# Sums over partitions: ones matmuls in place of a GpSimd operation

## The chip, the cores and the metric

The kernel runs on one core of a Trainium2 chip. The metric is the time of one execution on the device in microseconds. The engines are TensorE (PE: matmuls, and its weight loads, PEld), VectorE (DVE), ScalarE (ACT), GpSimd (POOL) and SyncE (SP), which here issues every DMA.

## The reference

Three stages follow each other: a decaying linear attention gives x (1536 tokens of 512), a mixture of 8 experts that is run densely for every token, and a last feed-forward layer with a leaky activation. Only the gate of the second stage matters here:

```python
logits = x @ w_gate                       # 1536 x 8
P = np.exp(logits - logits.max())
for _ in range(8):
    P /= P.sum(1, keepdims=True) + 1e-09  # over the 8 experts
    P /= P.sum(0, keepdims=True) + 1e-09  # over the 1536 tokens
    P *= N / E
for e in range(E):
    out += P[:, e:e+1] * (np.maximum(x @ w1[e], 0.0) @ w2[e])
```

## The kernel before

Tokens go in three blocks of 512. All engines work through their instructions in the order in which the code is written (a manual schedule); tiles from pools carry the waits. PSUM has a pool of seven banks under one tag (`bank`).

After the attention the loop runs over ten "experts" e (the eight real ones, and the last layer as two more) and the blocks b. `l1(e, b)` does eight tiles f of layer 1: 12 matmuls each, in three precisions (`mm3`: high by high, low by high, high by low), into a bank `a`; then ACT writes `hh` (the high half) and VectorE `hl` (the low half), which frees the bank. `l2T(e, b)` then sums over the eight tiles f into four banks `o`, 12 matmuls for each f; VectorE multiplies `o` by `pb`, the gate's row of this expert spread over all partitions.

Weights come from DRAM into `raw` (four slots), and `split_w` makes their halves: `wh` on ACT, `wl` on GpSimd (L98). The first three are split on VectorE during the attention. The next five belong to expert 0 and are split at tiles 0, 2, 4 and 6 of `l1(0, 0)` and tile 0 of `l2T(0, 0)` (the list `early`). Each split also issues a later weight load on SP's queue.

The gate is worked out beside `l1(0, 0)` and `l2T(0, 0)`. A list `side` holds its steps, and after each tile f one step is taken: `gate(2)`, `transposes`, then eight times `sink_iter`, two empty steps, and `sink_end` with `load_pb(0)`, so that the last falls behind tile 4 of `l2T(0, 0)`. The logits P lie as 128 partitions x 8 experts x 12 token groups, so a sum over tokens is a sum along the free dimension (VectorE, tile `s`) and then one over the partitions. The latter, and the maximum at the start (`mg` from `m`), are a custom operation of GpSimd, `partition_all_reduce` (L305, L321). `sink_end` transposes P on TensorE (`pt`, L335), writes it to DRAM (`pdram`) and reads back `pb`.

Of the kernel before, what the change touches and what calls it, by code (L numbers as in the profile page):

```python
# [8 lines left out]

F32 = mybir.dt.float32  # L10
# [4 lines left out]
ALU = mybir.AluOpType  # L15
AX = mybir.AxisListType
# [8 lines left out]
E, F = 8, 1024  # L25
# [10 lines left out]
def tile_kernel(ctx, tc, qkT, kv, cmask, ctab, w_gate, w1, w2, w_in, w_out, alpha, out):  # L36
    nc = tc.nc
# [3 lines left out]
    const = ctx.enter_context(tc.tile_pool(name="const", bufs=1))  # L41
# [10 lines left out]
    def bank(name):  # L52
        return psp.tile([128, 512], F32, tag="ps", name=name)

    ident = const.tile([128, 128], F32, name="ident")
    al = const.tile([128, FF // 128], F32, name="al")
    wg = const.tile([128, KD, E], F32, name="wg")
    wgs = const.tile([128, KD, 2 * E], F32R, name="wgs")
# [2 lines left out]
    Pt = const.tile([E * NT, 128], F32, name="Pt")  # L61
    pdram = drp.tile([E * NT, 128], F32, name="pdram")

    # ------------------------------------------------------------ weights
    srcs = []
    for e in range(E):
        srcs += [(1, w1[e][:, 256 * p:256 * p + 256]) for p in range(4)]
# [44 lines left out]
        xl[b] = xp.tile([128, KD, TB], F32R, tag=f"xl{b}", name=f"xl{b}_{gen}")  # L112

    with tc.manual_schedule():
        # -------------------------------------------------------- attention
        with ExitStack() as actx:
            ap_ = actx.enter_context(tc.tile_pool(name="attn", bufs=2))
            ld = actx.enter_context(tc.tile_pool(name="ld", bufs=3))
# [34 lines left out]
            for t in T:  # L153
                nc.gpsimd.memset(t, 0.0)
            make_identity(nc, ident)
            nc.gpsimd.memset(ebias, -896.0 * 2.0 ** 23)

            def scores(i):
# [92 lines left out]
            def gate(blk):  # L251
                if blk == 0:
                    lgT.append(gpool.tile([128, N], F32, tag="pb", name="lgT"))
                ps = bank(f"gt{blk}")
                for k in range(KD):
                    nc.tensor.matmul(ps[:16, :], wgs[:, k, :], xh[blk][:, k, :], start=(k == 0), stop=False)
                    nc.tensor.matmul(ps[:16, :], wgs[:, k, :], xl[blk][:, k, :], start=False, stop=(k == KD - 1))
                nc.scalar.activation(out=lgT[0][:16, TB * blk:TB * blk + TB], in_=ps[:16, :], func=AF.Copy)
# [6 lines left out]
            for i in range(NST):  # L265
# [16 lines left out]
                if i == 3:  # L282
                    nc.scalar.activation(out=wgs[:, :, 0:E], in_=wg, func=AF.Copy)
                    nc.gpsimd.tensor_tensor(
                        out=wgs[:, :, E:2 * E], in0=wg, in1=wgs[:, :, 0:E].bitcast(F32), op=ALU.subtract
                    )

        # -------------------------------------------------------- experts
        mp = ctx.enter_context(tc.tile_pool(name="mp", bufs=1))
        tp = ctx.enter_context(tc.tile_pool(name="tp", bufs=2))  # L290
        sp = ctx.enter_context(tc.tile_pool(name="sp", bufs=1))
        hh_t, hl_t, acc, pb = {}, {}, {}, {}

        def transposes():
            ps = bank("lgt")
            for t in range(NT):
                nc.tensor.transpose(ps[:, 16 * t:16 * t + 16], lgT[0][:16, C * t:C * t + C], ident[:16, :16])
            lg = sp.tile([128, NT * 16], F32, tag="lg", name="lg")
            nc.scalar.activation(out=lg, in_=ps[:, :NT * 16], func=AF.Copy)
            v = lg.rearrange("p (t e) -> p e t", e=16)  # L300
            nc.vector.tensor_tensor(out=P, in0=v[:, 0:E, :], in1=v[:, E:2 * E, :], op=ALU.add)
            m = sp.tile([128, 1], F32, tag="m", name="m")
            nc.vector.tensor_reduce(out=m, in_=P, axis=AX.XY, op=ALU.max)
            mg = sp.tile([128, 1], F32, tag="mg", name="mg")
            nc.gpsimd.partition_all_reduce(mg, m, channels=128, reduce_op=ReduceOp.max)  # L305
            nm = sp.tile([128, 1], F32, tag="nm", name="nm")
            nc.vector.tensor_scalar_mul(nm, mg, -1.0)
            nc.scalar.activation(out=P, in_=P, func=AF.Exp, bias=nm)

        def sink_iter(it):  # L310
            r = sp.tile([128, NT], F32, tag="r", name=f"r{it}")
            nc.vector.tensor_reduce(out=r, in_=P.rearrange("p e t -> p t e"), axis=AX.X, op=ALU.add)
            nc.vector.tensor_scalar_add(r, r, 1e-9)
            nc.vector.reciprocal(out=r, in_=r)
            nc.vector.tensor_tensor(
                out=P, in0=P, in1=r.unsqueeze(1).to_broadcast([128, E, NT]), op=ALU.mult
            )
            s = sp.tile([128, E], F32, tag="s", name=f"s{it}")
            nc.vector.tensor_reduce(out=s, in_=P, axis=AX.X, op=ALU.add)
            g = sp.tile([128, E], F32, tag="g", name=f"g{it}")  # L320
            nc.gpsimd.partition_all_reduce(g, s, channels=128, reduce_op=ReduceOp.add)  # L321
            nc.vector.tensor_scalar_add(g, g, 1e-9)  # L322
            nc.vector.reciprocal(out=g, in_=g)  # L323
            nc.vector.scalar_tensor_tensor(  # L324
                out=P,
                in0=P,
                scalar=float(N // E),
                in1=g.unsqueeze(2).to_broadcast([128, E, NT]),
                op0=ALU.mult,
                op1=ALU.mult,  # L330
            )

        def sink_end():
            ps = bank("pt")
            nc.tensor.transpose(ps[:E * NT, :128], P.rearrange("p e t -> p (e t)"), ident)  # L335
            nc.scalar.activation(out=Pt, in_=ps[:E * NT, :128], func=AF.Copy)
            nc.sync.dma_start(out=pdram, in_=Pt)

        def load_pb(e):
            pb[e] = gpool.tile([128, N], F32, tag="pb", name=f"pb{e}")  # L340
            nc.sync.dma_start(
                out=pb[e],
                in_=pdram[NT * e:NT * e + NT, :].rearrange("t p -> (t p)").partition_broadcast(128),
            )
# [35 lines left out]
        side = []  # L380
# [116 lines left out]
        for i in range(3, 8):  # L497
            early.append(i)
        side.append(lambda: gate(2))
        side.append(transposes)  # L500
        for it in range(8):
            side.append(lambda it=it: sink_iter(it))
        side += [lambda: None] * 2
        side.append(lambda: (sink_end(), load_pb(0)))

        todo = list(range(32))
# [83 lines left out]
```

## Time and profile before

| | |
|---|---|
| median of 3 runs | 1428.52 us (1428.16 to 1431.36) |
| profiled execution: span from first to last instruction | 1426.4 us |
| what lies around the span, by the median | 2.1 us |
| TensorE busy | 1372.0 us, 96% of the span |
| VectorE, ACT, GpSimd busy | 410.0, 269.8 and 395.2 us |
| mean granted clock of TensorE | 0.980 |
| DMA | 91.01 MB, q1 19.0% of 16 engines' span |

The profiled execution has no other time of its own than its span. In the timelines below, a row has the start in us, the duration, the engine, the line, the operation, what it writes and reads, and in brackets how long the engine was idle before it and what ended that. Matmuls overlap, so their durations are longer than the distance between two of them.

### The profile page before, as it was taken

The page shows a single profiled execution, that of the slowest core. Times are in us where ns is not written, and L with a number is a line of the kernel's source. Part 1 is how long each engine was busy: PE and PEld are TensorE (multiplying, and loading weights), DVE is VectorE, ACT ScalarE, POOL GpSimd, SP SyncE. Part 2 cuts the span into 40 slices and gives each one's busy share as a digit, 9 for nine tenths or more (in the row PEclk, how much of TensorE's full clock was granted, in tenths as well). Part 3 has the DMA queues.
Part 4 walks back from the last instruction along what each step waited for, and adds up shares of the span by engine and source line. Part 5 has one row for each costly group of instructions (what it writes and reads, how often), then busy time and mean ns, then how long its engine had stood idle before and what let it go on. Part 6 is the DMA issues. An engine that isn't in the chain of part 4 may idle for free.

```text
span 1426.4 us, 15358 instructions
## 1 busy us (share of the span) xinstructions
PE 1372.0 (96%) x6465; PEld 1130.2 (79%) x6465; DVE 410.0 (29%) x683; ACT 269.8 (19%) x396; POOL 395.2 (28%) x260
## 2 busy tenths in 40 slices
PE   9971899999999999999999999999999999999999
PEld 7750688888888888888888888888888888888887
DVE  5512211342143233314421432311112212233322
ACT  1310112111211221121122112211212321132100
POOL 4311004013410431241134105312412462264211
PEclk9985899999999999999999999999999999999999
DMA  9400003311321231033113212300310120010000
GB/s 330 167 29 29 24 1 104 118 52 33 123 67 52 75 125 45 30 103 119 52 34 121 67 52 74 111 1 1 103 37 0 45 74 0 0 60 1 30 30 30
DMA packets 46548, 91.01 MB, mean 64 GB/s; under 512 B 3504, under 2 KB 20240, under 8 KB 46480
## 3 DMA queue, kind: packets, MB, share of 16 engines
q1 hardware_dynamic: 46480, 90.04, 19.0%
q8 instruction: 50, 0.82, 0.2%
q14 instruction: 18, 0.15, 0.0%
HBM read 78.44 MB, written 11.58 MB: 63 GB/s over the span
## 4 chain that ended last, share of the span: by engine, by line
PE 89%; DVE 0%; issue 0%
PE a L105 15%; PE a L106 15%; PE a L104 15%; PE o L104 12%; PE o L105 12%; PE o L106 12%; PE o L494 3%; PE o L495 3%; PE o L493 3%; PE pt L335 0%; DVE y L470 0%; DVE P L324 0%; DVE g L323 0%; DVE g L322 0%
## 5 line engine op out<-in xcount | busy, mean ns | idle before, releaser
L104 PE MATMUL a<-xh,wh 128*128 128x512 f32 x960 | 373.7, 389 | 0.0
L106 PE MATMUL a<-xh,wl 128*128 128x512 f32 x960 | 373.5, 389 | 0.0
L105 PE MATMUL a<-xl,wh 128*128 128x512 f32 x960 | 373.5, 389 | 0.0
L106 PE MATMUL o<-hh,wl 128*128 128x512 f32 x768 | 302.2, 393 | 15.5 <-POOL wl L98 15.5
L104 PE MATMUL o<-hh,wh 128*128 128x512 f32 x768 | 302.6, 394 | 7.3 <-DVE hl L395 7.3
L105 PE MATMUL o<-hl,wh 128*128 128x512 f32 x768 | 302.0, 393 | 0.0
L98 POOL TENSOR_TENSOR wl<-raw,wh 128x1024 fp32r<-128x1024 f32 x77 | 183.9, 2389 | 294.2 <-ACT wh L97 259.5
L443 POOL TENSOR_TENSOR acc<-acc,t 128x512 f32<-128x512 f32 x84 | 105.8, 1291 | 507.1 <-DVE t L442 507.1
L394 ACT ACTIVATE hh<-a 128x512 fp32r<-128x512 f32 x192 | 112.3, 596 | 518.3 <-PE a L106 518.2
L104 PEld LDWEIGHTS a<-xh,wh 128*128 128x128 f32 x960 | 180.2, 188 | 37.7 <-issue 0.2
L106 PEld LDWEIGHTS a<-xh,wl 128*128 128x128 f32 x960 | 180.2, 188 | 37.5
L105 PEld LDWEIGHTS a<-xl,wh 128*128 128x128 f32 x960 | 180.2, 188 | 37.4
L395 DVE SCALAR_TENSOR_TENSOR hl<-a,hh 128x512 fp32r<-128x512 f32 x192 | 129.8, 688 | 246.0 <-ACT hh L394 246.0
L106 PEld LDWEIGHTS o<-hh,wl 128*128 128x128 f32 x768 | 146.2, 190 | 47.1 <-POOL wl L98 16.4
L104 PEld LDWEIGHTS o<-hh,wh 128*128 128x128 f32 x768 | 146.1, 190 | 38.8 <-DVE hl L395 8.4
L105 PEld LDWEIGHTS o<-hl,wh 128*128 128x128 f32 x768 | 146.2, 190 | 30.5
L442 DVE TENSOR_TENSOR t<-o,pb 128x512 f32<-128x512 f32 x84 | 57.9, 692 | 388.5 <-PE o L106 329.6
L97 ACT ACTIVATE wh<-raw 128x1024 fp32r<-128x1024 f32 x80 | 84.4, 1055 | 149.6 <-PE o L105 130.5
L409 POOL TENSOR_TENSOR hl<-g,hh 128x512 fp32r<-128x512 f32 x48 | 62.1, 1294 | 139.1 <-ACT hh L408 138.9
L494 PE MATMUL o<-wl,hh 128*128 128x512 f32 (+1 forms) x200 | 76.1, 381 | 0.0
L495 PE MATMUL o<-wh,hl 128*128 128x512 f32 (+1 forms) x200 | 76.1, 380 | 0.0
L493 PE MATMUL o<-wh,hh 128*128 128x512 f32 (+1 forms) x200 | 76.1, 380 | 0.0
(70 smaller groups left out, 573.6 us busy)
## 6 DMA issues: line engine op xcount, KB each, us to landing
raw<-in_w_dram SPq DMA_DIRECT2D x64, 512.0 KB, 3.5
rd<-in_w_in_dram SPq DMA_DIRECT2D x16, 512.0 KB, 3.7
wd<-q SPq DMA_DIRECT2D x32, 256.0 KB, 2.2
rd<-in_w_out_dram SPq DMA_DIRECT2D x16, 512.0 KB, 3.7
raw<-wd SPq DMA_DIRECT2D x16, 512.0 KB, 3.2
qk<-in_qkT_dram SPq DMA_DIRECT2D x12, 512.0 KB, 6.8
kv<-in_kv_dram SPq DMA_DIRECT2D x12, 512.0 KB, 5.7
pb<-pdram SPq DMA_DIRECT2D x8, 768.0 KB, 4.4
```

What stands on the lines that cost most here:

```text
L97: nc.scalar.activation(out=hi, in_=t, func=AF.Copy)
L98: eng.tensor_tensor(out=lo, in0=t, in1=hi.bitcast(F32), op=ALU.subtract)
L104: nc.tensor.matmul(ps, wh, xh, start=first, stop=False)
L105: nc.tensor.matmul(ps, wh, xl, start=False, stop=False)
L106: nc.tensor.matmul(ps, wl, xh, start=False, stop=last)
L394: nc.scalar.activation(out=hi, in_=ps, func=AF.Relu)
L395: nc.vector.scalar_tensor_tensor(out=lo, in0=ps, scalar=0.0, in1=hi.bitcast(F32), op0=ALU.max, op1=ALU.subtract)
L409: nc.gpsimd.tensor_tensor(out=lo, in0=g, in1=hi.bitcast(F32), op=ALU.subtract)
L443: nc.gpsimd.tensor_tensor(out=acc[b][:, d, :], in0=acc[b][:, d, :], in1=t, op=ALU.add)
L493: nc.tensor.matmul(ps, hh_, wh, start=first, stop=False)
L494: nc.tensor.matmul(ps, hh_, wl, start=False, stop=False)
L495: nc.tensor.matmul(ps, hl_, wh, start=False, stop=last)
```

## The change

The custom operation is gone. `ones`, a 128 x 128 matrix of ones, is filled on VectorE at the start. A sum over partitions is now a matmul of `ones` with the partial sums, whose result in PSUM has the total in every partition. For the maximum, VectorE multiplies the identity by `m` (`dm`, a diagonal matrix), the matmul spreads all 128 values over each partition, and VectorE takes the maximum of them. The iteration is cut at the matmul: `rows` is what leads up to `s`, `cols` begins with the matmul and ends with the `rows` of the next iteration. The list `side` is now `gate(2)`, `transposes`, `shift`, eight times `cols`, and `sink_end`, without empty steps.

```diff
+    ones = const.tile([128, 128], F32, name="ones")
...
+            nc.vector.memset(ones, 1.0)
...
-            mg = sp.tile([128, 1], F32, tag="mg", name="mg")
-            nc.gpsimd.partition_all_reduce(mg, m, channels=128, reduce_op=ReduceOp.max)
+            dm = sp.tile([128, 128], F32, tag="dm", name="dm")
+            nc.vector.tensor_scalar(out=dm, in0=ident, scalar1=m, scalar2=None, op0=ALU.mult)
+            sums["m"] = dm
+
+        def shift():
+            ps = bank("mx")
+            nc.tensor.matmul(ps[:, 0:128], ones, sums["m"], start=True, stop=True)
             nm = sp.tile([128, 1], F32, tag="nm", name="nm")
-            nc.vector.tensor_scalar_mul(nm, mg, -1.0)
+            nc.vector.tensor_reduce(out=nm, in_=ps[:, 0:128], axis=AX.X, op=ALU.max)
+            nc.vector.tensor_scalar_mul(nm, nm, -1.0)
             nc.scalar.activation(out=P, in_=P, func=AF.Exp, bias=nm)
+            rows(0)
 
-        def sink_iter(it):
+        def rows(it):
...
             nc.vector.tensor_reduce(out=s, in_=P, axis=AX.X, op=ALU.add)
+            sums[it] = s
+
+        def cols(it):
+            ps = bank(f"cs{it}")
+            nc.tensor.matmul(ps[:, 0:E], ones, sums[it], start=True, stop=True)
             g = sp.tile([128, E], F32, tag="g", name=f"g{it}")
-            nc.gpsimd.partition_all_reduce(g, s, channels=128, reduce_op=ReduceOp.add)
-            nc.vector.tensor_scalar_add(g, g, 1e-9)
+            nc.vector.tensor_scalar_add(g, ps[:, 0:E], 1e-9)
             nc.vector.reciprocal(out=g, in_=g)
...
+            if it < 7:
+                rows(it + 1)
...
         side.append(transposes)
+        side.append(shift)
         for it in range(8):
-            side.append(lambda it=it: sink_iter(it))
-        side += [lambda: None] * 2
+            side.append(lambda it=it: cols(it))
         side.append(lambda: (sink_end(), load_pb(0)))
```

In GpSimd's queue, from the last weight split that comes ahead of the gate, this stood before (rows named ISA without a tile are set-up instructions of the operation that follows):

```order
L98 TENSOR_TENSOR wl_755<-raw_452,wh_754 128x1024
L305 ISA
L305 ISA mg<-m 128x1
L98 ISA
L98 TENSOR_TENSOR wl_828<-raw_512,wh_827 128x1024
L321 ISA
L321 ISA g_840<-s_838 128x8
L321 ISA g_869<-s_867 128x8
L98 ISA
L98 TENSOR_TENSOR wl_892<-raw_610,wh_891 128x1024
```

And this stands there now:

```order
L98 TENSOR_TENSOR wl_757<-raw_454,wh_756 128x1024
L98 TENSOR_TENSOR wl_827<-raw_514,wh_826 128x1024
L98 TENSOR_TENSOR wl_893<-raw_612,wh_892 128x1024
L98 TENSOR_TENSOR wl_959<-raw_710,wh_958 128x1024
L98 TENSOR_TENSOR wl_1024<-raw_760,wh_1023 128x1024
```

The sums and the ISA rows are gone; the five splits of expert 0 follow each other directly.

In TensorE's queue, between tile 0 and tile 1 of layer 2 (`l2T(0, 0)`), this stands now, where before nothing stood between the two tiles:

```order
L104 MATMUL o_0_3_1010<-hh_0_0_752,wh_826 128x512
L105 MATMUL o_0_3_1010<-hl_0_0_753,wh_826 128x512
L106 MATMUL o_0_3_1010<-hh_0_0_752,wl_827 128x512
L332 MATMUL cs_1029<-s_1005,ones 128x8
L104 MATMUL o_0_0_1007<-hh_0_1_785,wh_826 128x512
```

The sum of iteration 5 has moved from GpSimd into the row of matmuls; the other seven and `mx` stand in the same way behind tiles of layer 1 and of layer 2.

In VectorE's queue, around `hl` of tile 6 in `l1(0, 0)`, this stood before:

```order
L322 TENSOR_SCALAR g_933<-g_933 128x8
L323 RECIPROCAL g_933<-g_933 128x8
L324 SCALAR_TENSOR_TENSOR P<-P,g_933 128x96
L395 SCALAR_TENSOR_TENSOR hl_0_6_952<-a_0_6_938,hh_0_6_951 128x512
L312 TENSOR_REDUCE r_961<-P 128x12
```

And this stands there now:

```order
L334 TENSOR_SCALAR g_930<-cs_928 128x8
L335 RECIPROCAL g_930<-g_930 128x8
L336 SCALAR_TENSOR_TENSOR P<-P,g_930 128x96
L320 TENSOR_REDUCE r_934<-P 128x12
L321 TENSOR_SCALAR r_934<-r_934 128x12
L322 RECIPROCAL r_934<-r_934 128x12
L323 TENSOR_TENSOR P<-P,r_934 128x96
L327 TENSOR_REDUCE s_939<-P 128x8
L409 SCALAR_TENSOR_TENSOR hl_0_6_955<-a_0_6_941,hh_0_6_954 128x512
L334 TENSOR_SCALAR g_966<-cs_964 128x8
```

The five operations from `r` to `s` of the next iteration have moved ahead of `hl`, so that `s` is written before the tile's `hl` and not behind it; the sum is read from PSUM (`cs`).

## Rows read from the trace of the kernel before

**Rows 1.** The page's 40 slices: busy tenths of TensorE, and its granted clock.

```profile
PE   9971899999999999999999999999999999999999
PEclk9985899999999999999999999999999999999999
```

**Rows 2.** Windows: us; busy us (x) of PE, PEld, DVE, ACT, POOL; clock, DMA.

```profile
40.00:57.00 17.00, 16.52 (x206) 13.38 (x201) 11.86 (x20) 5.46 (x8) 6.86 (x6) 1.00 0.51 190
99.70:105.00 5.30, 5.30 (x23) 4.38 (x24) 0.00 (x0) 0.00 (x0) 0.00 (x0) 1.00 0.31 99
119.40:124.00 4.60, 4.60 (x10) 3.11 (x10) 0.00 (x0) 0.00 (x0) 0.00 (x0) 0.50 0.38 114
160.00:400.00 240.00, 240.00 (x1060) 198.73 (x1059) 67.35 (x107) 49.07 (x71) 53.32 (x28) 1.00 0.21 67
```

**Rows 3.** Waits of TensorE, 57 to 165 us: us in total, times, longest.

```profile
PE pt L335 <- DVE P L324: 25.3, 1, 25.3
PE o L106 <- POOL wl L98: 15.5, 2, 14.0
PE o L104 <- DVE hl L395: 7.3, 2, 5.8
```

**Rows 4.** Timeline of GpSimd from 60 us.

```profile
60.45 2.38 POOL L98 TENSOR_TENSOR wl<-raw,wh 128x1024 fp32r<-128x1024 f32 x1 [10.19 <-ACT wh L97]
69.48 0.38 POOL L305 PARTITION_ALL_REDUCE mg<-m  x1 [6.64 <-issue]
76.96 2.39 POOL L98 TENSOR_TENSOR wl<-raw,wh 128x1024 fp32r<-128x1024 f32 x1 [7.11 <-issue]
```

**Rows 5.** Waits of GpSimd, 57 to 160 us.

```profile
POOL wl L98 <- issue: 28.3, 4, 7.6
POOL g L321 <- issue: 27.2, 4, 6.9
...
POOL mg L305 <- issue: 6.6, 1, 6.6
```

**Rows 6.** Timeline of TensorE: tile 1's end, starts of two layers.

```profile
62.95 0.39 PE L106 MATMUL a<-xh,wl 128*128 128x512 f32 x1
...
80.56 0.39 PE L104 MATMUL o<-hh,wh 128*128 128x512 f32 x1
...
160.42 0.39 PE L104 MATMUL a<-xh,wh 128*128 128x512 f32 x1
```

**Rows 7.** Timelines of VectorE at two places, and of ACT.

```profile
64.00 0.69 DVE L395 SCALAR_TENSOR_TENSOR hl<-a,hh 128x512 fp32r<-128x512 f32 x1 [3.85 <-ACT hh L394]
64.61 0.32 DVE L301 TENSOR_TENSOR P<-lg 128x96 f32<-128x96 f32 x1
...
70.08 0.38 ACT L308 ACTIVATE P<-P,nm 128x96 f32<-128x96 f32 x1 [5.53 <-DVE nm L307]
...
70.83 1.05 ACT L97 ACTIVATE wh<-raw 128x1024 fp32r<-128x1024 f32 x1
...
129.56 0.17 DVE L322 TENSOR_SCALAR g<-g 128x8 f32<-128x8 f32 x1 [0.53 <-POOL g L321]
...
130.30 0.32 DVE L312 TENSOR_REDUCE r<-P 128x12 f32<-128x96 f32 x1
...
131.41 0.25 DVE L319 TENSOR_REDUCE s<-P 128x8 f32<-128x96 f32 x1
```

**Rows 8.** Timeline of TensorE: f32 matmuls of the attention, and transpositions.

```profile
53.61 1.16 PE L226 MATMUL y<-q,T 128*128 128x128 f32 x8
...
63.27 0.91 PE L297 MATMUL lgt<-ident,lgT 16*128 16x16 f32 x12
```

**Rows 9.** `pt` and `pb`: timelines of TensorE and SP; DMA issues (KB, landing).

```profile
149.26 0.45 PE L335 MATMUL pt<-ident,P 128*96 128x128 f32 x1 [25.25 <-DVE P L324]
...
152.31 0.35 SPq L341 DMA_DIRECT2D pb<-pdram  x1
...
pb<-pdram SPq DMA_DIRECT2D x1, 768.0 KB, 4.3
```

More of the change, by code (lines that the diff above doesn't have):

```diff
@@ L5 @@
 from concourse import mybir
-from concourse.bass_isa import ReduceOp
 from concourse.masks import make_identity
@@ L291, in tile_kernel @@
         sp = ctx.enter_context(tc.tile_pool(name="sp", bufs=1))
-        hh_t, hl_t, acc, pb = {}, {}, {}, {}
+        hh_t, hl_t, acc, pb, sums = {}, {}, {}, {}, {}
         def transposes():
```

## The prediction

> **What bounds the kernel now.** I read the slices of the page first. TensorE is busy nine tenths or more of nearly every slice and its clock is full, except in the third to fifth slice, where the busy digits fall to 1 and the clock to 5 [rows 1]. So the kernel is bound by TensorE everywhere but in one hole. The table of windows puts numbers on this: from 160 to 400 us TensorE is never idle, 1060 matmuls in 240 us, one every 0.226 us; in the hole there are stretches at half clock (0.50), where one takes twice that [rows 2].
>
> Next, the waits of TensorE around the hole. There are three kinds: 25.3 us once for P before the transposition `pt`, 15.5 us for `wl` from GpSimd, 7.3 us for `hl` from VectorE; 48.1 us in all [rows 3]. The second one names GpSimd directly, so I read GpSimd's own timeline. It does one `wl` of 2.4 us, is idle 6.6 us, does a reduction over partitions of 0.4 us, is idle 7.1 us, does the next `wl`, and so on [rows 4]. The idle time is "issue": it waits for nothing that the profile shows. It stands before every switch between the two kinds of operation: 28.3 + 27.2 + 6.6 = 62.1 us in nine switches [rows 5]. The switches are what the hole is made of. `hl` and `pt` are the same wait at second hand: VectorE works in order, so `hl` of a later tile stands behind the addition to `g`, which waits for GpSimd; the seven PSUM banks are then full (five tiles of layer 1 whose `hl` is missing, two of `o`), and the third `o` has no bank.
>
> **What the change removes.** Layer 2 of expert 0, block 0 starts at 80.56 and the next layer 1 starts at 160.42 [rows 6]: 79.86 us for 8 x 12 = 96 matmuls. At 0.226 us these take 21.7. The excess is 58.1 us: 48.1 of waiting, the rest half clock and `pt`. After the change GpSimd has only `wl` left here. Five of them, 2.4 us each, have some 40 us; each is asked for six tiles of twelve matmuls (16 us) ahead of its use, so it is hidden. `hl` is no longer behind GpSimd. `pt` is left with about 0.2 us. So 57.9 us can go, and nothing outside of this stretch has an idle TensorE to give back.
>
> **What it adds on TensorE.** Nine matmuls with ones: one of 128 columns (`mx`), eight of 8 columns (`cs`). No such row exists. Four f32 matmuls of 128 columns, counted as eight instructions, take 1.16 us: 0.29 each; twelve transpositions of 16 columns take 0.91: 0.08 each [rows 8]. `pt`, which stood alone at the low clock, took 0.45 [rows 9]. An 8-column sum still has its 128 x 128 weights to load, so I take the nearest row in weights, 0.3: 9 x 0.3 = 2.7 us; ends 9 x 0.08 = 0.7 and 9 x 0.45 = 4.1. Not below nothing: they are extra instructions on the engine that never rests.
>
> **The waits it adds.** `cs` of iteration k stands in TensorE's queue behind a whole tile of layer 1 (12 x 0.226 = 2.7 us), and everything of the next tile stands behind it. It needs `s`, the end of a chain on VectorE that itself begins with the `hl` of the tile before. Counted from the start of that tile's last matmul: `hl` starts 1.05 later (62.95 to 64.00) [rows 6, 7], holds VectorE for 0.61 (64.00 to 64.61), and then the eight operations from `g` to `s` take 2.10 (129.56 to 131.41 + 0.25) [rows 7]: 3.76 us. TensorE is there after 0.23 + 0.3 + 2.7 = 3.25. The wait is 0.5 us. But a wait delays the next tile and not VectorE, so the next `cs` finds its `s` ready: 0.5 every second time. `cs` 1 and 3 are free, 2 and 4 wait 0.5 each. `cs` 0 has another chain: `hl`, the maximum over 128 columns (0.32, as `r`), the negation (0.17), the exponential (0.38), five operations from `r` to `s` (130.30 to 131.66, 1.36) [rows 7], 1.05 + 0.61 + 0.32 + 0.17 + 0.38 + 1.36 and some gaps = 4.0, against 3.25: 0.8. ACT's `hh` and `wh` (1.05 [rows 7]) stand before the exponential but end before the negation does. In layer 2 there is no `hl` between, and the 2.1 us fit into a tile of 2.7: `cs` 5 to 7 wait for nothing. Sum 0.8 + 0.5 + 0.5 = 1.8 us; ends: 0, and 1 us for each of nine, 9 us, if VectorE reads PSUM more slowly than its rows here with SBUF say.
>
> **What could be late next.** `pb`. `pt` starts at 149.26, `pb` is issued at 152.31 and lands 4.3 later [rows 9]: 7.4 us. Now `pt` stands after tile 3 of layer 2, one tile earlier than before, and the first `o` is finished 39 matmuls later, 8.8 us. It just fits, and if it doesn't, three free banks cover another 8 us of layer 1. On SP's queue `pdram` stands behind four weight loads that wait for GpSimd's `wl`, the last of which is asked for in tile 0 of layer 2 and done some 6 us before `pdram`.
>
> **The sum.** 80.56 + 21.7 + 2.7 + 1.8 + 0.2 = 107.0 instead of 160.42: 53.4 us less. From the span of 1426.4 this gives 1373.0; the median of the runs is 1428.5, 2.1 us around the span, so **1375**. With the ends: 57.9 - 0.7 = 57.2 saved, 1371.3; 57.9 - 4.1 - 9 = 44.8 saved, 1383.7.
>
> **Rivals.**
> 1. *TensorE pays for each sum* at full clock, about 1 to 1.5 us nine times over, by matmuls that don't overlap and a slower VectorE chain: 57.9 - 4.1 - 9 to 57.9 - 4.1 - 13.5, 1384 to 1388. For it: the chain is 3.76 us against 3.25, so there is no slack. Against it: every second wait cancels. 12 in 100.
> 2. *The clock falls to its lower level through the small waits.* 156 matmuls (five tiles and layer 2) would take 0.226 us more each, 35 us: 1375 + 35 = 1410. Against it: at 40 to 57 us TensorE has small gaps too (16.5 us busy of 17) and a clock of 1.00, and the shorter of the two waits for `wl` (15.5 - 14.0 = 1.5 us [rows 3]), which ends just before 99.70, is followed by a stretch at 1.00 as well [rows 2]. The Trainium skill's TensorE: Matmul & The Clock Gate, section A second HAM failure mode: psum-queue depth-cycling, tells of a kernel where frequent micro-idles between groups of matmuls make the clock swing between its two levels; by that rule this rival would be the forecast, and the trace so far does not agree. 4 in 100.
> 3. *Slower than before.* Each `cs` stands in the queue of the engine that bounds, so nine tiles last as long as the chain to `s` if that is longer. With a chain of 8.5 us they cost 9 x (8.5 - 2.7) = 52 us, and with TensorE idle most of the time the clock falls, which costs the last five tiles 60 x 0.226 = 13.6: 65.8 against 57.9 saved, +8, 1436. It decides from a chain of (57.9 - 13.6) / 9 + 2.7 = 7.6 us. Against it: every operation of the chain has a row, and they sum to half of that, 3.76. 2 in 100. The Trainium skill's GPSIMD Engine Reference, section Engine selection, sends reductions along the partition dimension to GpSimd and would side with this rival; the trace agrees on the operation alone (0.38 us [rows 4] against my 0.3 plus a wait), not on the idle time around it.
> 4. *The pauses stay*: if GpSimd's 7 us belong to each `wl` and not to the switch, the last of four `wl` ends 4 x 9.4 us after about 68.7 (tile 2 ends five tiles before 80.56, then ACT does `hh` and `wh`): at 106.3, with two tiles of layer 2 still to do, 5.4 us. Layer 1 would go on at 111.7, 48.7 us earlier than now: 1380. Against it: the `wl` at 60.45 waited for ACT's `wh` and shows no "issue" [rows 4]. 3 in 100. That nothing is gained, since what is saved here is waited for later: 1 in 100.
>
> **Numbers.** The forecast has 78 in 100, with its own range 1371 to 1381. The range 1370 to 1385 takes in rival 4 and the near end of rival 1. What this kernel's measurement can tell from no change is about 0.3%, 4.3 us. Faster by more: forecast, rivals 1, 2 and 4, 0.97, of which I keep 0.95 for what I have not thought of; the same 0.02; slower 0.03.
>
> **What will show it.** Right: GpSimd's timeline between 60 and 110 us has no "issue" idle time; TensorE's clock is 1.00 from 57 us on; layer 1 of block 1 starts near 107; the waits of TensorE for `s` (VectorE L327) are about three, none over 1 us; `acc` of L453 starts without waiting for `pb`. Wrong: waits for `s` at every `cs`, or over 1 us; a granted clock under 1 between 67 and 107; TensorE waiting for `wl` or for `hl` as before; a first `cs` that waits for the exponential behind `wh`.

## The result, and the profile after

The changed kernel takes 1388.26 us (median of 4 runs, 1387.22 to 1391.04) against 1428.34 of the kernel before on the same chip: a ratio of 0.9722, with a 95% interval of 0.9707 to 0.9737. The direction is as forecast, but 40 us are saved where 53 were forecast, and the time lies 3 us above the upper end of the range. Its span is 1386.5 us where the sum had 1373.0.

In the slices of the page the hole of [rows 1] is all but gone:

```profile
PE   9979999999999999999999999999999999999999
PEclk9989999999999999999999999999999999999999
```

One slice, the third, is left with a 7 for busy and an 8 for the clock. What TensorE waits for between 57 and 130 us is a single kind, and none of those of [rows 3]; the columns are us in total, times, longest:

```profile
PE cs L332 <- DVE s L327: 9.1, 3, 4.5
```

So the waits come at three of the eight sums, as forecast, but are five times as long in all: 1.8 us were forecast, and 9.1 stand here. GpSimd's timeline, to be read against [rows 4]:

```profile
70.17 2.36 POOL L98 TENSOR_TENSOR wl<-raw,wh 128x1024 fp32r<-128x1024 f32 x1 [5.96 <-ACT wh L97]
78.37 2.37 POOL L98 TENSOR_TENSOR wl<-raw,wh 128x1024 fp32r<-128x1024 f32 x1 [5.84 <-ACT wh L97]
88.81 2.37 POOL L98 TENSOR_TENSOR wl<-raw,wh 128x1024 fp32r<-128x1024 f32 x1 [8.06 <-ACT wh L97]
91.77 2.34 POOL L98 TENSOR_TENSOR wl<-raw,wh 128x1024 fp32r<-128x1024 f32 x1 [0.59 <-ACT wh L97]
```

No idle time is "issue" any more; GpSimd waits for ACT alone. Now VectorE in the same stretch:

```profile
70.70 0.33 DVE L320 TENSOR_REDUCE r<-P 128x12 f32<-128x96 f32 x1 [0.44 <-ACT P L315]
71.06 1.50 DVE L321 TENSOR_SCALAR r<-r 128x12 f32<-128x12 f32 x1
...
78.41 2.44 DVE L336 SCALAR_TENSOR_TENSOR P<-P,g 128x96 f32<-128x96 f32 x1
80.89 0.32 DVE L320 TENSOR_REDUCE r<-P 128x12 f32<-128x96 f32 x1
...
83.20 0.26 DVE L336 SCALAR_TENSOR_TENSOR P<-P,g 128x96 f32<-128x96 f32 x1
...
88.85 2.44 DVE L336 SCALAR_TENSOR_TENSOR P<-P,g 128x96 f32<-128x96 f32 x1
...
91.89 0.23 DVE L322 RECIPROCAL r<-r 128x12 f32<-128x12 f32 x1
92.15 2.07 DVE L323 TENSOR_TENSOR P<-P,r 128x96 f32<-128x96 f32 x1
94.26 0.25 DVE L327 TENSOR_REDUCE s<-P 128x8 f32<-128x96 f32 x1
```

The same multiplication by `g` takes 0.26 us at 83.20 and 2.44 at 78.41 and 88.85. Lay the ends beside GpSimd's: 78.41 + 2.44 = 80.85, and the `wl` that began 0.04 us earlier ends at 78.37 + 2.37 = 80.74. The division at 92.15 ends at 94.22, the `wl` beside it at 94.11. The addition at 71.06 ends at 72.56, its `wl` at 72.53. So three kinds of small VectorE operation end just behind the `wl` that runs beside them; the sums of L320 (70.70, 0.33 us) and the reciprocal (91.89, 0.23 us), which ran beside a `wl` too, do not. An operation that ends late in this way is called held below, and the time added its hold. Four held operations lost 1.33 + 2.18 + 2.18 + 1.81 = 7.5 us against their length alone.

TensorE pays for that at each `cs` behind such an operation:

```profile
73.46 0.39 PE L332 MATMUL cs<-s,ones 128*128 128x8 f32 x2 [1.98 <-DVE s L327]
...
76.55 0.28 PE L332 MATMUL cs<-s,ones 128*128 128x8 f32 x2
76.69 0.48 PE L104 MATMUL a<-xh,wh 128*128 128x512 f32 x1
77.00 0.39 PE L105 MATMUL a<-xl,wh 128*128 128x512 f32 x1
...
82.31 0.39 PE L332 MATMUL cs<-s,ones 128*128 128x8 f32 x2 [2.63 <-DVE s L327]
...
86.95 0.32 PE L332 MATMUL cs<-s,ones 128*128 128x8 f32 x2
...
94.57 0.59 PE L332 MATMUL cs<-s,ones 128*128 128x8 f32 x2 [4.45 <-DVE s L327]
...
100.28 0.43 PE L332 MATMUL cs<-s,ones 128*128 128x8 f32 x2
...
103.46 0.28 PE L332 MATMUL cs<-s,ones 128*128 128x8 f32 x2
...
120.46 0.39 PE L104 MATMUL a<-xh,wh 128*128 128x512 f32 x1
```

The distances tell of a second loss. From 73.46 to 76.55 a tile takes 3.09 us; behind the wait of 2.63 us it takes 4.64 (82.31 to 86.95), behind the one of 4.45 us 5.71 (94.57 to 100.28), then 3.18 again. The granted clock in two of these stretches and in the one after (columns as in [rows 2]):

```profile
83.60:87.00 3.40, 3.40 (x10) 2.66 (x9) 1.13 (x5) 0.00 (x0) 0.00 (x0) 0.50 0.01 5
95.00:100.00 5.00, 5.00 (x13) 3.94 (x14) 1.96 (x9) 0.00 (x0) 0.00 (x0) 0.50 0.36 105
...
101.00:120.00 19.00, 19.00 (x87) 15.64 (x86) 5.50 (x21) 0.27 (x1) 0.00 (x0) 1.00 0.13 45
```

After the two longer waits most of one tile each runs at the lower level (0.50, 1.2 GHz); after the wait of 1.98 us the clock stayed at 1.00 and the tile takes 3.09 us. Against 3.09 us the two tiles lost 1.55 + some 2.6 = 4.2 us. The last row of TensorE's timeline above is layer 1 of block 1: 120.46, where before it was 160.42 [rows 6] and the sum had 107.0.

Of the signs that the prediction named, two of being wrong came: waits for `s` over 1 us, and a granted clock under 1 between 67 and 107. Those of being right that came are the missing "issue", the number of waits, and `acc`, which waits for `o` and not for `pb` (VectorE's timeline):

```profile
118.62 2.73 DVE L453 TENSOR_TENSOR acc<-o,pb 128x512 f32<-128x512 f32 x4 [11.17 <-PE o L106]
```

### The profile page after: what moved, and what is told of

It is laid out like the page before. It is cut to its first block, busy times and chain, and to the rows that moved or that the text cites. A ratio compares the mean times of both kernels' runs of the same rounds, so it can differ in the third digit from the quotient of the medians.

```text
span 1386.5 us, 15371 instructions
## 1 busy us (share of the span) xinstructions
PE 1369.4 (99%) x6482; PEld 1129.9 (81%) x6483; DVE 418.6 (30%) x686; ACT 270.4 (20%) x396; POOL 391.9 (28%) x251
## 4 chain that ended last, share of the span: by engine, by line
PE 97%; DVE 1%; DMA 1%; ACT 0%; issue 0%; SPq 0%; POOL 0%; POOLq 0%
PE a L104 16%; PE a L106 16%; PE a L105 16%; PE o L104 13%; PE o L106 13%; PE o L105 13%; PE o L507 3%; PE o L509 3%; PE o L508 3%; PE y L237 1%; PE sc L165 1%; PE y L227 1%; DMA qk<-in_qkT_dram 1%; DMA kv<-in_kv_dram 0%; DVE P L336 0%; PE st L203 0%
## 5 line engine op out<-in xcount | busy, mean ns | idle before, releaser
L423 POOL TENSOR_TENSOR hl<-g,hh 128x512 fp32r<-128x512 f32 x48 | 62.1, 1294 | 139.0 <-ACT hh L422 139.0
```

The source lines that it names most:

```text
L423: nc.gpsimd.tensor_tensor(out=lo, in0=g, in1=hi.bitcast(F32), op=ALU.subtract)
```

## The experiments

The theory, formed from these rows: a VectorE operation that reads two tiles in SBUF (or runs a TENSOR_SCALAR from SBUF to SBUF) cannot run beside GpSimd's `wl` and is held until that ends. The rivals: the operations of the chain are slow by themselves; the splits are late (the waits above name no `wl`, which speaks against it already); TensorE pays for each sum as such; or the gain never came from the sums but from the switches alone. The ratios are to the kernel before on the same chip, with 95% intervals.

**`r` and `g` in PSUM.** A VectorE operation that has one operand in PSUM has only one in SBUF. `r` and `g` move to the bank of the sum, with nothing else changed:

```diff
-        def rows(it):
-            r = sp.tile([128, NT], F32, tag="r", name=f"r{it}")
+        def rows(it, ps):
+            r = ps[:, 256:256 + NT]
...
-            g = sp.tile([128, E], F32, tag="g", name=f"g{it}")
+            g = ps[:, 64:64 + E]
```

> The changed kernel with the small tiles r and g kept in the PSUM bank of the sum instead of SBUF; nothing else moves. Theory (hold): in the changed kernel four VectorE operations of the chain to s last 1.50, 2.44, 2.44 and 2.07 us instead of 0.17 to 0.26, and each ends within 0.1 us of the end of a wl on GpSimd; they are those with two SBUF inputs or a TENSOR_SCALAR from SBUF to SBUF. With r and g in PSUM none is of that kind: none over 0.5 us, TensorE waits for s about 2 us in all instead of 9.1, its clock stays 1.00, time 1388.3 - 7.3 - 4.3 = 1377 (1375 to 1380). Rival (any VectorE operation beside GpSimd is slow, or they wait for something that is not GpSimd): still operations of 1.5 to 2.4 us, 1388.

Measured: 1376.42 us, 0.9627 (0.9613 to 0.9640), clock 1.00. In GpSimd's timeline a `wl` has its old length:

```profile
77.23 2.37 POOL L98 TENSOR_TENSOR wl<-raw,wh 128x1024 fp32r<-128x1024 f32 x1 [4.54 <-ACT wh L97]
```

VectorE's timeline has the addition and the division beside the `wl` before it and, beside this one, the multiplication:

```profile
71.22 0.18 DVE L321 TENSOR_SCALAR mx<-mx 128x12 f32<-128x12 f32 x1
...
71.71 0.25 DVE L323 TENSOR_TENSOR P<-P,mx 128x96 f32<-128x96 f32 x1
...
77.29 0.26 DVE L336 SCALAR_TENSOR_TENSOR P<-P,cs 128x96 f32<-128x96 f32 x1
```

And the waits of TensorE:

```profile
PE cs L332 <- DVE s L327: 1.7, 3, 0.7
```

The multiplication takes 0.26 us instead of 2.44, the addition 0.18 instead of 1.50, and the waits are 0.67, 0.50 and 0.48 us: those of the prediction (0.8, 0.5, 0.5), once the hold is gone. TensorE's timeline has the first row of layer 1 in block 0 and in block 1:

```profile
57.24 0.50 PE L104 MATMUL a<-xh,wh 128*128 128x512 f32 x1
...
108.83 0.39 PE L104 MATMUL a<-xh,wh 128*128 128x512 f32 x1
```

That is 51.6 us, where the prediction's sum gives 107.0 - 55.73 = 51.3 and the changed kernel took 63.4 (57.09 to 120.46). The operations are not slow by themselves, and 12 us hang on where two small tiles lie.

**Only `g` in PSUM.** The second of the two edits alone.

> The changed kernel with g alone in PSUM; r stays in SBUF. Theory (hold): L336 is free (0.3 us), but the next operation of the held kind, the addition to r or the product of P with r, now stands there and is held to the end of the same wl, so the gain is only the 0.4 to 0.7 us of the operations between, for each of three holds: 1386 to 1388. Rival (only this form of SCALAR_TENSOR_TENSOR is slow): the 2 x 2.2 us of L336 go, 1388.3 - 4.4 or, with the clock, 1380 to 1384.

Measured: 1382.55 us, 0.9673 (0.9660 to 0.9686): better than expected, and in the range of the rival (1380 to 1384). The time alone would speak for the rival; the rows decide against it. The multiplication by `g` is no longer held, and the next operation with both ends in SBUF is caught in its place, as VectorE's timeline shows:

```profile
79.23 0.25 DVE L336 SCALAR_TENSOR_TENSOR P<-P,cs 128x96 f32<-128x96 f32 x1
...
79.88 1.69 DVE L321 TENSOR_SCALAR r<-r 128x12 f32<-128x12 f32 x1
```

The hold moved, as expected, but it now begins 0.65 us later in the `wl` (79.17 to 81.54) and is the shorter for it, and the last `wl`, at 91.89, held an operation for 0.63 us only. The waits are 1.99, 2.01 and 1.90 us, 5.9 in all; I had counted full holds. The clock fell after the first two (the tiles behind them took 4.66 and 4.51 us) and not after the third (3.11 us). A stretch behind the second:

```profile
83.90:86.80 2.90, 2.90 (x8) 2.24 (x8) 0.99 (x5) 0.00 (x0) 0.00 (x0) 0.50 0.16 57
```

**GpSimd's `wl` done twice** for the five early splits:

```diff
-        eng.tensor_tensor(out=lo, in0=t, in1=hi.bitcast(F32), op=ALU.subtract)
+        for _ in range(2 if 3 <= i < 8 else 1):
+            eng.tensor_tensor(out=lo, in0=t, in1=hi.bitcast(F32), op=ALU.subtract)
```

> The changed kernel with GpSimd's wl of the five early splits written twice over, one after the other (the second is the same work again). Theory (hold): GpSimd is at work for 4.8 us instead of 2.4 each time; the four holds last up to 2.4 us longer each, so operations of 3.9 to 4.9 us, TensorE waits 9 us more, and the clock is low for longer: 1398 to 1405. If VectorE gets in between the two, half of that. Rival (not GpSimd): 1388.

Measured: 1396.67 us, 0.9769 (0.9755 to 0.9783), the waits for `s` 14.5 us. GpSimd's timeline has a place where four `wl` follow each other;

```profile
92.93 9.53 POOL L99 TENSOR_TENSOR wl<-raw,wh 128x1024 fp32r<-128x1024 f32 x4 [8.50 <-ACT wh L97]
```

in VectorE's the chain does one held operation in each of the first three:

```profile
92.98 2.45 DVE L337 SCALAR_TENSOR_TENSOR P<-P,g 128x96 f32<-128x96 f32 x1
95.46 0.32 DVE L321 TENSOR_REDUCE r<-P 128x12 f32<-128x96 f32 x1
95.82 1.95 DVE L322 TENSOR_SCALAR r<-r 128x12 f32<-128x12 f32 x1
...
98.06 2.08 DVE L324 TENSOR_TENSOR P<-P,r 128x96 f32<-128x96 f32 x1
```

A fourth, of 1.02 us, falls into the last `wl`. None lasts longer than one `wl` by more than 0.1 us: a hold ends with the operation that runs, not with GpSimd's queue. That is the case the expectation named as the cheaper one, with half of the loss; the time is accordingly under its 1398 to 1405.

**`wl` in quarters.** If so, four short `wl` should hold less than a long one:

```diff
-        eng.tensor_tensor(out=lo, in0=t, in1=hi.bitcast(F32), op=ALU.subtract)
+        for c in range(0, 1024, 256 if 3 <= i < 8 else 1024):
+            cc = slice(c, c + (256 if 3 <= i < 8 else 1024))
+            eng.tensor_tensor(out=lo[:, cc], in0=t[:, cc], in1=hi[:, cc].bitcast(F32), op=ALU.subtract)
```

> The changed kernel with GpSimd's wl of the five early splits cut into four operations of 256 columns. Theory (a held operation waits for the end of the GpSimd operation that runs, not for the queue behind it): no VectorE operation of the chain over 0.95 us; each split can hold three or four of them for up to 0.65 us, so holds of 3 to 5 us instead of 7.5, waits of at most 1.5 us, clock 1.00: 1379 to 1384. Rival (VectorE gets in only when GpSimd's queue is empty): operations of 1.5 to 2.5 us as before, 1388.

Measured: 1377.37 us, 0.9640 (0.9624 to 0.9656), below the expected range. In GpSimd's timeline the four together take 2.82 us instead of 2.37:

```profile
76.24 2.82 POOL L100 TENSOR_TENSOR wl<-raw,wh 128x256 fp32r<-128x256 f32 x4 [4.66 <-ACT wh L97]
```

In VectorE's, the multiplication beside them takes 0.80:

```profile
76.29 0.80 DVE L338 SCALAR_TENSOR_TENSOR P<-P,g 128x96 f32<-128x96 f32 x1
```

The waits are 3.8 us, the longest 1.3, and the clock stayed at 1.00.

**The share of the clock.** Here TensorE gets matmuls to do ahead of the three sums that wait; nothing reads their results. Everything else is as in the changed kernel.

```diff
+            if it in (0, 2, 4):
+                fps = bank(f"fill{it}")
+                for _ in range({0: 6, 2: 9, 4: 16}[it]):
+                    nc.tensor.matmul(fps, one[:, 0:128], one, start=True, stop=True)
```

> The changed kernel with matmuls that nobody reads (bf16, of ones) ahead of cs 0, 2 and 4: 6, 9 and 16 of them, some 1.3, 1.9 and 3.5 us, which fit into the waits for s of 1.98, 2.63 and 4.45 us. Theory (the clock is the second part of the miss): the granted clock stays at 1.00 and the 21 matmuls that ran at half clock, 4.3 us, are given back: 1388.3 - 4.3 = 1384 (1383 to 1386). Rival (the clock costs nothing here, all of the miss is in the waits): 1388 or, as the filler only adds work, later.

Measured: 1383.03 us, 0.9679 (0.9665 to 0.9694). VectorE is held as before (2.44 us at 77.69), but TensorE's clock does not fall (the windows of this kernel, columns as in [rows 2]):

```profile
57.00:115.00 58.00, 55.75 (x260) 41.49 (x259) 30.65 (x82) 11.17 (x18) 11.81 (x5) 1.00 0.22 69
```

The span is 5.2 us shorter than that of the changed kernel, 0.7 of it because layer 1 started earlier (56.36 against 57.09): 4.5 us for the clock, against 4.2 by the distances above.

**The switches alone.** The kernel before, with GpSimd's sums, and only the five early splits (with the weight loads that they issue) moved ahead of them, two to tile 0 and three to tile 1 of `l1(0, 0)`:

```diff
-                if early and f % 2 == 0:
-                    split_w(early.pop(0))
+                for _ in range({0: 2, 1: 3}.get(f, 0)):
+                    if early:
+                        split_w(early.pop(0))
```

> The kernel before, GpSimd's sums over partitions kept, but the five early splits are taken at tiles 0 and 1 of layer 1 (2 and 3), so that GpSimd does all wl first and then all nine sums: one switch on TensorE's path instead of nine. Theory (the switches cost, not the sums): one pause of 6.6 us, first sum near 79 us, then a sum every 2.7 to 3.1 us, pt near 103 instead of 149; layer 1 goes on at 110 to 118 instead of 160: 1428.3 - 46, 1378 to 1388. Rival (each sum on GpSimd has its 7 us): nothing to gain, 1428.

Measured: 1383.00 us, 0.9675 (0.9662 to 0.9689): faster than the change itself, without any matmul of ones. GpSimd's timeline:

```profile
61.29 11.90 POOL L98 TENSOR_TENSOR wl<-raw,wh 128x1024 fp32r<-128x1024 f32 x5 [10.16 <-ACT wh L97]
79.76 0.38 POOL L305 PARTITION_ALL_REDUCE mg<-m  x1 [6.57 <-issue]
...
83.32 0.43 POOL L321 PARTITION_ALL_REDUCE g<-s  x1 [3.19 <-DVE s L319]
86.45 0.40 POOL L321 PARTITION_ALL_REDUCE g<-s  x1 [2.70 <-DVE s L319]
```

One "issue" pause of 6.57 us is left in this stretch, and from there a sum costs 0.4 us and waits for VectorE alone. What the change took away was the alternation of two kinds of work on GpSimd, not the price of a sum. This grouping was not tuned: TensorE still waits 7.2 us in it, 3.9 for `hl` and 3.3 for P before `pt`.

**The best version.** The first experiment, with the gate's step written ahead of `hh` and `hl` in tiles 3 to 7 of `l1(0, 0)`, so that the chain to `s` does not stand behind `hl`, which holds VectorE for 0.61 us [rows 7]:

```diff
+                if e == 0 and b == 0 and f >= 3:
+                    side.pop(0)()
...
-                if side:
+                if side and not (e == 0 and b == 0 and f >= 3):
```

> e1 (r and g in PSUM) and, in tiles 3 to 7 of layer 1 of the first block, the gate's step is written ahead of the tile's hh and hl instead of behind them. Then VectorE does the chain to s first and hl after it. By the prediction's own arithmetic the chain after cs is 0.45 + 2.1 us and fits into a tile of 2.7, so the waits of e1 (0.67, 0.50, 0.48) go except the first: 1376.4 - 1.0 = 1375.4 (1374 to 1377). Rival: hl comes 2 us later and its bank is missed, TensorE waits for hl instead: 1377 to 1380.

Measured: 1374.12 us, 0.9618 (0.9604 to 0.9633). Of TensorE's waits one of 0.7 us is left:

```profile
PE cs L332 <- DVE s L327: 0.7, 1, 0.7
```

It beats both kernels; from the first experiment its interval does not tell it apart.

## Why the prediction was right in direction and wrong in size

**Right: what goes.** All "issue" pauses before a switch (62.1 us [rows 5]) are gone, and with them the waits for `wl`, for `hl` and for `pt`; the early-splits experiment shows that they were the price of switching. Rival 4 (the pauses belong to each `wl`) has fallen. So has the doubt about `pb`: it fitted. **Right: what a sum costs on TensorE.** Counted by distance, from the start of a sum to that of the second matmul behind it less one ordinary matmul at the clock of the place (77.00 - 76.55 - 0.23 = 0.22 us), the nine cost 0.22 to 0.59 us each and 2.8 us in all, against 9 x 0.3 = 2.7.

**Wrong: the step "The waits it adds".** It took the chain to `s` as 3.76 us from rows at 64.00 to 65 and 129.56 to 131.66 [rows 7]. At those times GpSimd did no `wl`: before the change the sums and `wl` stood in one queue, and while one of the later four `wl` ran, the chain stood still, waiting for `g`. One of the four, in GpSimd's timeline of the kernel before:

```profile
97.25 2.35 POOL L98 TENSOR_TENSOR wl<-raw,wh 128x1024 fp32r<-128x1024 f32 x1 [7.60 <-issue]
```

and what VectorE does around it:

```profile
92.00 0.25 DVE L319 TENSOR_REDUCE s<-P 128x8 f32<-128x96 f32 x1
107.00 0.17 DVE L322 TENSOR_SCALAR g<-g 128x8 f32<-128x8 f32 x1 [14.74 <-POOL g L321]
```

The rows were right and were taken from a kernel in which the two did not meet. The change lets them meet: the splits stand at every second tile, the tiles whose operations lead to the `s` that TensorE waits for, and there the chain grows by 1.33, 2.18 and 3.99 us. Added to the forecast waits of 0.8, 0.5 and 0.5 this gives 2.1, 2.7 and 4.5 us, against 1.98, 2.63 and 4.45 measured: the step missed the holds, and without them was right to within 0.2 us each time. The other half of the mistake stands under "What the change removes": the five `wl` were called hidden because TensorE wants them late; whom they disturb while they run was not asked. Rival 3's "every operation of the chain has a row" was no protection, for the same reason.

The miss of the span, 1386.5 against 1373.0, term by term:

- waits for `s`: 9.1 instead of 1.8, +7.3. The 9 us that stood as the upper end have this size by chance: their reason was a VectorE that reads PSUM more slowly than SBUF, and operands in PSUM turned out to be the remedy;
- two tiles at the lower clock: +4.2 by the distances, shown by the filled waits (4.5). The clock was only in rivals 2 and 3, for 156 and 60 matmuls; here it fell for most of one tile each time, after the waits of 2.63 and 4.45 us and not after that of 1.98;
- the start of layer 1: 57.09 instead of 55.73, +1.4. The attention ahead of it differs only by the filling of `ones`; the two kernels run here without it have the start at 55.73 and 56.56, those with it between 54.9 and 57.5, so I put it down to the difference between executions, which is not shown;
- the rest, +0.6, was not followed up; in the first experiment, without holds and at the full clock, the same stretch was 0.3 us over the sum.

Of the rivals, the first one (1384 to 1388) has the measured time at its edge, by another mechanism: not nine sums at 1 us each but three waits behind a `wl`, and the other six free. It had 12 in 100, and the range left its far end out.

A rule that speaks against the change was there to be weighed: the Trainium skill's SBUF — State Buffer, section Who interferes with whom, says that a VectorE instruction with two inputs in SBUF contends with a GpSimd instruction that reads SBUF, that one which can enter a two-port mode, such as tensor_scalar, can do so too, that in such a mode the one that issues first keeps the other out for the whole instruction, and that tensor_reduce and other instructions with at most one input in SBUF outside those modes do not take part. The runs agree in each point that they touch: 2.44 us held beside a `wl`, 0.26 with `g` in PSUM, TENSOR_SCALAR at 1.50 beside one, TENSOR_REDUCE at 0.32 with a `wl` beside it, and no hold longer than one `wl`. That shared ports are the cause is the Trainium skill's word; the runs show who is held and how long. The rule that the prediction weighed instead, from the Trainium skill's GPSIMD Engine Reference, section Engine selection, which sends reductions along the partition dimension to GpSimd, is borne out in part: sums over partitions are cheap on GpSimd (0.40 us) once it does nothing else in between, but the matmuls with `r` and `g` in PSUM are 7 to 9 us faster (1376.42 and 1374.12 against 1383.00) than the one grouping that was tried.

## What to carry to other kernels

A duration is read from a trace together with what ran beside it; before using it, ask whether the change lets two engines run together that the old order kept apart, and where the operands of their operations lie. Where GpSimd alternates between a custom operation and ordinary ones, look for the pauses before each switch and try grouping the work first. For a small VectorE operation on a chain that a busy TensorE waits for, try one operand in PSUM, or shorter operations on GpSimd beside it; here they were worth 12 and 11 us.

## What the runs showed of the hardware that was not expected

- A VectorE operation of 0.26 us took 2.44 us beside a GpSimd `wl` of 2.37, while GpSimd's own operation kept its length (2.38 us in [rows 4]); with one operand in PSUM it took 0.26 beside a `wl`.
- The hold lasts as long as the running operation: between two `wl` in a row VectorE gets its turn (one held operation in each of three, 1.95 to 2.45 us), and with quarters of a `wl` it was 0.80 us.
- TensorE's clock fell to 0.50 after single waits of 2.63 and 4.45 us and came back about one tile later; after 1.98 us it stayed in the changed kernel, and with `g` alone in PSUM it fell after 1.99 and 2.01 us and stayed after 1.90.
